# The last kv head's output-projection rows split into two 24-partition loads and one small load, in a one-core decode kernel

## The chip, the core and the metric

The kernel runs on one core of one Trainium2 chip. The metric is the device time of one execution in microseconds (us). The kernel before takes 124.86 us, the median of three runs (124.79 to 124.87).

## The reference

One decode step for a batch of 8, with one token each (D = 512). Cut to what matters:

```python
xn = layernorm(x)
q  = (xn @ wq)                        # 32 query heads of 128, 8 kv heads (4 query heads each)
k, v = last 1024 rows of each cache   # W = max(256, Sk // 4), Sk = 4096
s  = (softmax(q k^T / sqrt(128)) v) @ wo              # [8, 4096] @ [4096, 512]
g  = silu((gelu(xn @ w_gate) * (xn @ w_up)) @ w_down) # F = 1792
out = x + s * g
```

All inputs are bf16. The caches are read only in their last 1024 rows, 32 MB for K and V together; the weights are about 14 MB. The output is 8 x 512.

## The kernel before

Everything is written out in one order by hand, and every engine runs its own instructions in that order.

**Loads.** All large loads are issued on SyncE's queue (SP) into the slots of one ring of 19 tiles of 128 partitions x 8 KB (`slot`, L81). `load_rows` (L84 to 92) brings wq in four loads, w_gate and w_up in two each, w_down in two. `load_set` (L94 to 103) brings one set, that is four batches of one kv head, of K or of V, 1 MB. There are 16 sets. `load_wo` (L105 to 114) brings the 512 rows of wo that belong to one kv head: partition p gets rows 4p to 4p+3 of the head, so the four rows of a partition are one run of memory. Eight counters take turns for the landings, so a load is issued only when the load eight before it has landed.

**Order of the loads.** wq, w_gate, w_up, K of sets 0 to 2, w_down, then V and K in turns, and at the end wo: seven heads in one load of 512 KB each, the eighth in two halves of 256 KB (L473 and 474).

**Work.** The main loop (L434 on) is in quarters of a set. TensorE transposes K (L292), VectorE and ScalarE copy it out of PSUM by turns (L297, L299), TensorE forms the scores (L309), the maxima are taken out (L318 to L343), ScalarE takes the exponentials (L349), TensorE forms the sums and the product with V (L354, L371), and VectorE scales the result into `oT` (L377): partition = element d of a head, then kv head h, query head j, batch b.

**pick and put.** wo's rows for a head are in order 128j + d. With `load_wo`, partition p holds rows 4p + r, so `oT` has to be reordered to match. `pick` (L388 to 396) does it for one kv head with four matmuls by 0/1 matrices `picks[r]` into a PSUM tile `m_ps`; `put` (L398 to 404) copies the four blocks of 32 partitions into `oR`. Both run for each head one step after its last product with V, for the last head after everything else.

**Constants.** GpSimd builds the 0/1 matrices ahead of everything by `select` (L132, an affine select). Its last work is to clear `xq_sb` (L180); four small loads of x on ScalarE's queue (L183) wait for that.

**End.** After the loop VectorE clears `s_ps` (L472), and TensorE multiplies `oR` with wo (L479): for each of the four r of each head, four matmuls, one for each block of 128 output columns, each into its own block of 32 partitions of `s_ps`. 128 matmuls in all. Then two VectorE operations (L488, L489) and four small stores (L492).

Of the kernel before, what the change touches and what calls it, by code (L numbers as in the profile page):

```python
# [9 lines left out]
ALU = mybir.AluOpType  # L10
AX = mybir.AxisListType
BF16 = mybir.dt.bfloat16
FP32 = mybir.dt.float32
# [4 lines left out]
def kernel(  # L18
# [13 lines left out]
    nc = tc.nc  # L32

    B, Sq, D = A_x.shape
    Hkv, Sk, Dh = A_k_cache.shape[1], A_k_cache.shape[2], A_k_cache.shape[3]
    Hq = A_wq.shape[1] // Dh
    rep = Hq // Hkv
# [6 lines left out]
    P = nc.NUM_PARTITIONS  # L44
# [10 lines left out]
    QT = 4  # L55
    CQ = NCH // QT
    NQB = D // 128
    NEG = -1.0e30
    SHK = 64 + G

    consts = ctx.enter_context(tc.tile_pool(name="consts", bufs=1))
    ring = ctx.enter_context(tc.tile_pool(name="ring", bufs=19))
    kT_pool = ctx.enter_context(tc.tile_pool(name="kT_pool", bufs=8))
    pT_pool = ctx.enter_context(tc.tile_pool(name="pT_pool", bufs=6))
    small = ctx.enter_context(tc.tile_pool(name="small", bufs=3))
    rows = ctx.enter_context(tc.tile_pool(name="rows", bufs=1))
# [6 lines left out]
    ps_m = ctx.enter_context(tc.tile_pool(name="ps_m", bufs=1, space=PSUM))  # L73
# [7 lines left out]
    def slot():  # L81
        return ring.tile([P, SET], BF16, name="slot")

    def load_rows(w, r0, n, per, name):  # L84

        t = slot()
        cols = w.shape[1]
        nc.sync.dma_start(  # L88
            out=t[:, 0 : n * cols],
            in_=w.rearrange("(p k) n -> p k n", p=P)[:, r0 : r0 + n, :],  # L90
        )
        return t[:, 0 : n * cols].rearrange("p (k n) -> p k n", k=n)
# [12 lines left out]
    def load_wo(h, r0, n):  # L105

        t = slot()
        nc.sync.dma_start(
            out=t[:, 0 : n * D],
            in_=A_wo[h * rep * Dh : (h + 1) * rep * Dh, :].rearrange(  # L110
                "(p r) n -> p r n", r=rep
            )[:, r0 : r0 + n, :],
        )
        return t[:, 0 : n * D].rearrange("p (r n) -> p r n", r=n)

    wq_tiles = [load_rows(A_wq, k, 1, NDC, "wq") for k in range(NDC)]


    ident = consts.tile([P, P], BF16, name="ident")
    identf = consts.tile([P, P], FP32, name="identf")  # L120
    ones = consts.tile([P, P], BF16, name="ones")
    zsrc = consts.tile([P, P], FP32, name="zsrc")
# [9 lines left out]
    def select(out, in_, op, fill, base, pattern, cm):  # L132
        nc.gpsimd.affine_select(
            out=out, in_=in_, compare_op=op, fill=fill, base=base,
            pattern=pattern, channel_multiplier=cm,
        )
# [14 lines left out]
    for r in range(rep):  # L151
        t = consts.tile([P, P], BF16, name=f"pick{r}")
# [3 lines left out]
    for i in range(3):  # L156
        t = consts.tile([P, NC], BF16, name=f"shift{i}")
# [9 lines left out]
        shifts.append(t)  # L167


    stats = rows.tile([B, nc.vector.BN_STATS_DIM], FP32, name="stats")  # L170
    nc.vector.bn_stats(out=stats, in_=x_sb)
    mv = rows.tile([B, nc.vector.BN_AGGR_DIM], FP32, name="mv")
# [9 lines left out]
    for q in range(NQB):  # L182
        nc.scalar.dma_start(  # L183
            out=xq_sb[32 * q : 32 * q + B, :],
            in_=x_flat[:, q * 128 : (q + 1) * 128],
# [4 lines left out]
        out=xhat, in0=x_sb, scalar1=mv[:, 0:1], scalar2=rstd[:, 0:1],  # L190
# [10 lines left out]
    qT = rows.tile([P, Hkv, B, rep], BF16, name="qT")  # L201
    oT = rows.tile([P, Hkv, rep, B], BF16, name="oT")
    oR = rows.tile([P, Hkv, rep, B], BF16, name="oR")
    hT = rows.tile([P, NFC, B], BF16, name="hT")
    g_sb = rows.tile([P, 128], FP32, name="g_sb")

# [2 lines left out]
    for k in range(NDC):  # L209
        w = wq_tiles[k]  # L210
        for m in range(Hq):
            nc.tensor.matmul(  # L212
                q_ps[:, m, :], w[:, 0, m * Dh : (m + 1) * Dh], xnT[:, k, :],
                start=(k == 0 and m == 0), stop=(k == NDC - 1 and m == Hq - 1),
                skip_group_check=True,
            )
    nc.vector.tensor_copy(
        out=qT, in_=q_ps.rearrange("p (h j) b -> p h b j", j=rep)
# [5 lines left out]
    for w, src in enumerate((B_w_gate, B_w_up)):  # L224
        for k0 in range(0, NDC, KW):
            wt = load_rows(src, k0, KW, NDC, "gu")
            wv = wt.rearrange("p k (f j) -> p k j f", j=NFC)
            for j in range(NFC):
                for k in range(KW):
                    nc.tensor.matmul(  # L230
                        gu_ps[:, j, w, :], wv[:, k, j, :], xnT[:, k0 + k, :],
                        start=(w == 0 and k0 == 0 and j == 0 and k == 0),
                        stop=(w == 1 and k0 + k == NDC - 1 and j == NFC - 1),
                        skip_group_check=True,
# [54 lines left out]
    def transpose_quarter(s, i):  # L289
        ps = ps_kT.tile([P, CQ * P], BF16, name="kT_ps")  # L290
        for c in range(CQ):
            nc.tensor.transpose(  # L292
                ps[:, c * P : (c + 1) * P], K[s][:, i * CQ + c, :], ident
            )
        t = kT_pool.tile([P, CQ * P], BF16, name="kT")
        if i % 2 == 0:
            nc.vector.tensor_copy(out=t, in_=ps)  # L297
        else:
            nc.scalar.activation(out=t, in_=ps, func=ACT.Copy)  # L299
        kT[s, i] = t  # L300

    def score_quarter(s, i):
        h, b0 = s // NB, (s % NB) * G
        if i == 0:
            sc[s] = ps_sc.tile([P, NCH, NC], FP32, name="sc")
        t = kT.pop((s, i))
        q = qT[:, h, b0 : b0 + G, :].rearrange("p b j -> p (b j)")
        for c in range(CQ):
            nc.tensor.matmul(  # L309
                sc[s][:, i * CQ + c, :], t[:, c * P : (c + 1) * P], q,  # L310
                start=(i == 0 and c == 0), stop=False, skip_group_check=True,
            )
# [28 lines left out]
    def exponentials(s):  # L341
        r = shifts[s % 3]
        nc.tensor.matmul(  # L343
            sc[s].rearrange("p c n -> p (c n)"), spread[0:SHK, :],
            r[0:SHK, :].unsqueeze(1).to_broadcast([SHK, NCH, NC]),
            start=False, stop=True, skip_group_check=True,
# [38 lines left out]

    picked = {}

    def pick(h):  # L388
        ps = ps_m.tile([P, rep, rep, B], FP32, name="m_ps")
        for r in range(rep):  # L390
            nc.tensor.matmul(  # L391
                ps[:, r, :, :].rearrange("p j b -> p (j b)"), picks[r],
                oT[:, h, :, :].rearrange("p j b -> p (j b)"),
                start=(r == 0), stop=(r == rep - 1), skip_group_check=True,
            )
        picked[h] = ps

    def put(h):  # L398
        ps = picked.pop(h)
        for j in range(rep):  # L400
            nc.vector.tensor_copy(  # L401
                out=oR[32 * j : 32 * j + 32, h, :, :],
                in_=ps[32 * j : 32 * j + 32, :, j, :],
            )
# [15 lines left out]
    def fetch(kind, s):  # L420
        while True:
            k, i = pending.pop(0)
            if k == "K":
                K[i] = load_set(A_k_cache, i)
            elif k == "V":
                V[i] = load_set(A_v_cache, i)
            else:
                n = NFC // 2
                down_tiles.append(load_rows(B_w_down, i * n, n, NFC, "wd"))
            if (k, i) == (kind, s):  # L430
                return

    LV = 4 * (AHEAD - 1) + 2
    for t in range(QT * NS + LV + QT + 3):  # L434
        s, i = divmod(t, QT)
        if s < NS:
            if i == 0:
                fetch("K", s)
            transpose_quarter(s, i)
        s2, i2 = divmod(t - 2, QT)  # L440
        if 0 <= s2 < NS:
            score_quarter(s2, i2)
            if i2 == QT - 1:
                maxima(s2)
        u = t - 6
        if u >= 0 and u % QT == 0 and u // QT < NS:
            max_rows(u // QT)
        u = t - 8
        if u >= 0 and u % QT == 0 and u // QT < NS:
            exponentials(u // QT)  # L450
        u = t - 11
        if u >= 0 and u % QT == 0 and u // QT < NS:
            sums(u // QT)
        s3, i3 = divmod(t - LV, QT)
        if 0 <= s3 < NS:
            if i3 == 0:
                fetch("V", s3)
            value_quarter(s3, i3)
        u = t - LV - 2 * QT - 1
        if u >= 0 and u % (2 * QT) == 0:  # L460
            pick(u // (2 * QT))
        if u > 0 and u % (2 * QT) == 1:
            put(u // (2 * QT))
        if t == QT * AHEAD + 1:
            down(0)
        if t == QT * AHEAD + 3:
            down(1)
            gate()


    s_ps = ps_s.tile([P, 128], FP32, name="s")
    nc.vector.memset(s_ps, 0.0)  # L472
    parts = [(h, 0, rep) for h in range(Hkv - 1)]  # L473
    parts += [(Hkv - 1, 0, rep // 2), (Hkv - 1, rep // 2, rep // 2)]
    for h, r0, n in parts:
        w = load_wo(h, r0, n)
        for r in range(r0, r0 + n):
            for q in range(NQB):
                nc.tensor.matmul(  # L479
                    s_ps[32 * q : 32 * q + B, :], oR[:, h, r, :],  # L480
                    w[:, r - r0, q * 128 : (q + 1) * 128],
                    start=(h == 0 and r == 0), stop=(h == Hkv - 1 and r == rep - 1),
                    skip_group_check=True,
                )
    tmp = small.tile([P, 128], FP32, name="tmp", bufs=1)
    out_sb = small.tile([P, 128], BF16, name="out_sb", bufs=1)
    o_flat = out.flatten_outer_dims()
# [2 lines left out]
    for q in range(NQB):  # L490
        eng = nc.sync if q % 2 == 0 else nc.scalar
        eng.dma_start(  # L492
            out=o_flat[:, q * 128 : (q + 1) * 128], in_=out_sb[32 * q : 32 * q + B, :]
# [31 lines left out]
```

## Time and profile before

| What | Value |
|---|---|
| median of three runs | 124.86 us |
| the profiled execution | 124.77 us |
| its span in the profile | 123.0 us |
| DMA in the chain that ended last | 87% |
| read from HBM | 47.46 MB, 386 GB/s over the span |
| TensorE busy | 89.6 us (73%) |
| VectorE busy | 69.1 us (56%) |
| ScalarE busy | 45.9 us (37%) |
| GpSimd busy | 4.9 us (4%) |
| granted TensorE clock, mean | 0.936 |

Times inside the profile count from the span's start. The profiled execution's own time is 1.77 us longer than its span. The chain that ended last is followed back from the last instruction: a large share for DMA says that the end waits for loads. PE is TensorE's matmuls, PEld its weight loads, DVE VectorE, ACT ScalarE, POOL GpSimd, SP SyncE. A core has 16 DMA engines, and the DMA share is the mean over them.

### The profile page before, as it was taken

The numbers are of one execution on the slowest core, as the hardware profiler recorded it, in microseconds if no ns is written. First come the engines' busy times: TensorE is split into PE (matmuls) and PEld (weight loads), VectorE is DVE, ScalarE is ACT, GpSimd is POOL, SyncE is SP. The second block draws the span as 40 slices with busy tenths as digits, with TensorE's granted clock in tenths as the row PEclk, the third lists the DMA queues.
The fourth block names the chain that finished last, engine by engine and source line by source line (L and its number), as shares of the span: only waits on it lengthen the run. The fifth ranks groups of instructions, "written<-read, shape, count | busy, mean of one in ns | idle before, by whom it ended". The sixth has DMA issues, their size and how long they took to land.

```text
span 123.0 us, 4592 instructions
## 1 busy us (share of the span) xinstructions
PE 89.6 (73%) x2044; PEld 80.5 (65%) x2044; DVE 69.1 (56%) x218; ACT 45.9 (37%) x54; POOL 4.9 (4%) x21
## 2 busy tenths in 40 slices
PE   0243368868995799998979798767979779854840
PEld 0243358858984698988879697666968768643720
DVE  3400100043676547998787796669679689876010
ACT  4000000073583507567466355445536545510000
POOL 6800000000000000000000000000000000000000
PEclk9999999999999859999999999999999999995555
DMA  4999999999999999999999999999999999999720
GB/s 115 426 426 416 423 417 421 425 410 423 423 420 410 426 418 416 413 413 418 426 410 421 413 426 416 418 416 416 416 426 405 424 416 421 401 408 407 306 82 3
DMA packets 7508, 47.77 MB, mean 388 GB/s; under 512 B 952, under 2 KB 960, under 8 KB 2880
## 3 DMA queue, kind: packets, MB, share of 16 engines
q1 hardware_dynamic: 7376, 47.46, 93.7%
q8 instruction: 16, 0.26, 0.9%
q10 hardware_dynamic: 112, 0.02, 0.2%
q14 instruction: 4, 0.03, 0.1%
HBM read 47.46 MB, written 0.01 MB: 386 GB/s over the span
## 4 chain that ended last, share of the span: by engine, by line
DMA 87%; PE 8%; issue 1%; DVE 1%; SPq 1%; DVEq 0%
DMA slot<-in_A_k_cache_dram 49%; DMA slot<-in_A_wo_dram 23%; DMA slot<-in_B_w_up_dram 8%; DMA slot<-in_A_wq_dram 7%; PE kT_ps L292 3%; PE s L268 1%; PE sc L309 1%; PE o_ps L371 1%; SPq L88 1%; PE sc L343 0%; PE s L479 0%; DVE tmp L488 0%; DVE out_sb L489 0%; PE m_ps L325 0%; PE sum_ps L354 0%
## 5 line engine op out<-in xcount | busy, mean ns | idle before, releaser
L292 PE MATMUL kT_ps<-ident,slot 128*128 128x128 bf16 x512 | 41.9, 229 | 7.5 <-DMA slot<-in_A_k_cache_dram 6.0
L299 ACT ACTIVATE kT<-kT_ps 128x1024 bf16<-128x1024 bf16 x32 | 32.7, 1023 | 23.6 <-PE kT_ps L292 22.0
L292 PEld LDWEIGHTS <-slot 128*128 128x128 bf16 x512 | 31.8, 102 | 9.2 <-DMA slot<-in_A_k_cache_dram 7.5
L297 DVE COPY kT<-kT_ps 128x1024 bf16<-128x1024 bf16 x32 | 21.7, 679 | 9.7 <-PE kT_ps L292 9.7
L371 PEld LDWEIGHTS <-slot 128*128 128x128 bf16 x512 | 20.4, 96 | 7.9 <-issue 2.5
L371 PE MATMUL o_ps<-pT,slot 128*128 128x16 bf16 x512 | 22.0, 170 | 2.1 <-DVE oT L377 1.2
L309 PE MATMUL sc<-qT,kT 128*128 128x16 bf16 x512 | 22.5, 171 | 0.0
L309 PEld LDWEIGHTS <-kT 128*128 128x128 bf16 x512 | 19.9, 97 | 0.0
L349 ACT ACTIVATE pT<-sc 128x512 bf16<-128x512 f32 x16 | 9.6, 597 | 16.4 <-PE sc L343 16.3
L318 DVE TENSOR_REDUCE mx<-sc 128x16 f32<-128x512 f32 x16 | 11.1, 691 | 4.6 <-PE sc L309 4.3
L359 DVE TENSOR_REDUCE rec<-sum_ps 128x16 f32<-128x512 f32 x16 | 11.1, 691 | 3.9 <-PE sum_ps L354 3.5
L230 PE MATMUL sc<-xnT,slot 128*128 128x8 bf16 x112 | 7.4, 202 | 3.4 <-DMA slot<-in_B_w_gate_dram 2.7
L230 PEld LDWEIGHTS <-slot 128*128 128x128 bf16 x112 | 7.0, 159 | 3.7 <-DMA slot<-in_B_w_gate_dram 2.9
L241 ACT ACTIVATE z<-sc 128x112 f32<-128x112 f32 x1 | 0.3, 263 | 20.8 <-PE sc L230 20.8
L212 PE MATMUL sc<-xnT,slot 128*128 128x8 bf16 x128 | 4.1, 169 | 4.9 <-DMA slot<-in_A_wq_dram 4.9
L212 PEld LDWEIGHTS <-slot 128*128 128x128 bf16 x128 | 3.7, 104 | 5.3 <-DMA slot<-in_A_wq_dram 5.3
L354 PE MATMUL sum_ps<-pT,ones 128*128 128x512 bf16 x16 | 6.1, 379 | 0.5 <-issue 0.5
L401 DVE CAST oR<-m_ps 32x32 bf16<-32x32 f32 x32 | 5.8, 183 | 0.7 <-PE m_ps L391 0.4
L479 PE MATMUL s<-slot,oR 128*8 128x128 bf16 x128 | 4.3, 305 | 2.7 <-DMA slot<-in_A_wo_dram 1.5
L242 DVE TENSOR_SCALAR z<-z 128x112 f32<-128x112 f32 x1 | 0.2, 219 | 10.6 <-ACT z L241 10.6
L343 PE MATMUL sc<-shift,spread 68*128 68x512 bf16 x16 | 6.0, 376 | 0.2
L325 PE MATMUL m_ps<-identf,mx 128*16 128x128 f32 x16 | 4.5, 283 | 2.1 <-DVE mx L318 1.2
(58 smaller groups left out, 47.8 us busy)
## 6 DMA issues: line engine op xcount, KB each, us to landing
slot<-in_A_k_cache_dram SPq DMA_DIRECT2D x16, 1024.0 KB, 14.9
slot<-in_A_v_cache_dram SPq DMA_DIRECT2D x16, 1024.0 KB, 20.1
slot<-in_A_wq_dram SPq DMA_DIRECT2D x4, 1024.0 KB, 10.4
slot<-in_A_wo_dram SPq DMA_DIRECT2D x7, 512.0 KB
slot<-in_B_w_gate_dram SPq DMA_DIRECT2D x2, 896.0 KB
slot<-in_B_w_up_dram SPq DMA_DIRECT2D x2, 896.0 KB
slot<-in_B_w_down_dram SPq DMA_DIRECT2D x2, 896.0 KB
slot<-in_A_wo_dram SPq DMA_DIRECT2D x2, 256.0 KB, 9.4
```

The lines of the kernel that those rows point to most:

```text
L212: nc.tensor.matmul(q_ps[:, m, :], w[:, 0, m * Dh : (m + 1) * Dh], xnT[:, k, :], start=(k == 0 and m == 0), stop=(k == NDC - 1 and m == Hq ...
L230: nc.tensor.matmul(gu_ps[:, j, w, :], wv[:, k, j, :], xnT[:, k0 + k, :], start=(w == 0 and k0 == 0 and j == 0 and k == 0), stop=(w == 1 an ...
L292: nc.tensor.transpose(ps[:, c * P : (c + 1) * P], K[s][:, i * CQ + c, :], ident)
L297: nc.vector.tensor_copy(out=t, in_=ps)
L299: nc.scalar.activation(out=t, in_=ps, func=ACT.Copy)
L309: nc.tensor.matmul(sc[s][:, i * CQ + c, :], t[:, c * P : (c + 1) * P], q, start=(i == 0 and c == 0), stop=False, skip_group_check=True,)
L318: nc.vector.tensor_reduce(out=m, in_=sc[s].rearrange("p c n -> p n c"), axis=AX.X, op=ALU.max)
L343: nc.tensor.matmul(sc[s].rearrange("p c n -> p (c n)"), spread[0:SHK, :], r[0:SHK, :].unsqueeze(1).to_broadcast([SHK, NCH, NC]), start=Fal ...
L349: nc.scalar.activation(out=t, in_=sc.pop(s), func=ACT.Exp, scale=scale)
L354: nc.tensor.matmul(ps.rearrange("p c n -> p (c n)"), ones, pT[s].rearrange("p c n -> p (c n)"), start=True, stop=True,)
L359: nc.vector.tensor_reduce(out=t, in_=ps.rearrange("p c n -> p n c"), axis=AX.X, op=ALU.add)
L371: nc.tensor.matmul(o_ps[s].rearrange("p g j -> p (g j)"), V[s][:, c, :], pT[s][:, c, :], start=(c == 0), stop=(c == NCH - 1),)
```

## The change

The ring has 18 slots in place of 19, and a tile `wlow` of 64 partitions x 8 KB is added.

For the last head (`LAST`), the 128 rows of each query head j are divided: rows d = 0 to 31 and rows d = 32 to 127.

- `load_wo_low` loads rows 32 to 127 of all four j, three quarters of the head, in two loads of 24 partitions each: partitions 0 to 23 and 32 to 55 of `wlow`. Partition 32g + 4e + j holds the eight rows 32 + 48g + 8e to 39 + 48g + 8e of query head j, 8 KB in one run. The outer dimension of the source is e, six long.
- `load_wo_few` loads rows 0 to 31 of all four j, 128 rows of 1 KB, one on each partition of a ring slot.
- The order at the end is: heads 0 to 5 in one load each, the two low loads of the last head, head 6 in two halves, and the few rows of the last head.
- `pick_last` brings `oT` of the last head into the matching order with 36 matmuls in place of four: for the few rows and for each of the eight rows of a partition one matmul for each j, by a slice of `few` (132 columns) or of `spots[r]` (60 columns), 128 or 56 columns wide, that starts at column 3 - j. `put` then makes two copies in place of four: into the new tile `oL` (56 partitions x 64) and into `oR`.
- The product with wo has 148 matmuls in place of 128.
- GpSimd builds `few` and eight `spots`, and clears `wlow`, ahead of clearing `xq_sb`.

```diff
+    DF = 32
+    NE = 6
+    RL = (Dh - DF) // (2 * NE)
+    PL = 32 + rep * NE
+    LAST = Hkv - 1
-    ring = ctx.enter_context(tc.tile_pool(name="ring", bufs=19))
+    ring = ctx.enter_context(tc.tile_pool(name="ring", bufs=18))
...
+    def load_wo_few(h):
+        t = slot()
+        nc.sync.dma_start(
+            out=t[:, 0:D],
+            in_=A_wo[h * rep * Dh : (h + 1) * rep * Dh, :].rearrange(
+                "(j d) n -> d j n", j=rep
+            )[0:DF],
+        )
+        return t[:, 0:D].rearrange("p (r n) -> p r n", r=1)
+    wlow = rows.tile([P // 2, RL * D], BF16, name="wlow")
+    def load_wo_low(h):
+        t = wlow
+        rows_h = A_wo[h * rep * Dh : (h + 1) * rep * Dh, :].rearrange(
+            "(j d) n -> j d n", j=rep
+        )[:, DF:Dh, :]
+        for g in range(2):
+            nc.sync.dma_start(
+                out=t[32 * g : 32 * g + rep * NE, 0 : RL * D],
+                in_=rows_h[:, g * NE * RL : (g + 1) * NE * RL, :].rearrange(
+                    "j (e r) n -> e j (r n)", e=NE
+                ),
+            )
+        return t[0 : 32 + rep * NE, 0 : RL * D].rearrange("p (r n) -> p r n", r=RL)
...
+    few = consts.tile([P, P + rep], BF16, name="few")
+    nc.gpsimd.memset(few, 0.0)
+    select(
+        few[:, rep - 1 : P + rep - 1 : rep], zsrc[:, 0:DF], ALU.not_equal, 1.0, 0,
+        [[-1, DF]], 1,
+    )
+    spots = []
+    for r in range(RL):
+        t = consts.tile([P, PL + rep], BF16, name=f"spot{r}")
+        nc.gpsimd.memset(t, 0.0)
+        for g in range(2):
+            c0 = 32 * g + rep - 1
+            select(
+                t[:, c0 : c0 + rep * NE : rep], zsrc[:, 0:NE], ALU.not_equal, 1.0,
+                -(DF + NE * g * RL + r), [[-RL, NE]], 1,
+            )
+        spots.append(t)
+    nc.gpsimd.memset(wlow, 0.0)
...
+    oL = rows.tile([PL, RL, B], BF16, name="oL")
...
+    def pick_last(h):
+        ps = ps_m.tile([P, RL + 1, B], FP32, name="m_ps")
+        for r in [RL, *range(RL)]:
+            lo, n = (few, P) if r == RL else (spots[r], PL)
+            for j in range(rep):
+                nc.tensor.matmul(
+                    ps[0:n, r, :], lo[:, rep - 1 - j : n + rep - 1 - j], oT[:, h, j, :],
+                    start=(r == RL and j == 0), stop=(r == RL - 1 and j == rep - 1),
+                    skip_group_check=True,
+                )
+        picked[h] = ps
...
     def put(h):
         ps = picked.pop(h)
+        if h == LAST:
+            nc.vector.tensor_copy(out=oL[:, :, :], in_=ps[0:PL, 0:RL, :])
+            nc.vector.tensor_copy(out=oR[:, h, 0, :], in_=ps[:, RL, :])
+            return
...
-            pick(u // (2 * QT))
+            h = u // (2 * QT)
+            (pick_last if h == LAST else pick)(h)
...
-    parts = [(h, 0, rep) for h in range(Hkv - 1)]
-    parts += [(Hkv - 1, 0, rep // 2), (Hkv - 1, rep // 2, rep // 2)]
+    half = rep // 2
+    parts = [(h, 0, rep) for h in range(Hkv - 2)]
+    parts += [(LAST, 1, RL), (Hkv - 2, 0, half), (Hkv - 2, half, half), (LAST, 0, 1)]
+    done, total = 0, (Hkv - 1) * rep + RL + 1
     for h, r0, n in parts:
-        w = load_wo(h, r0, n)
-        for r in range(r0, r0 + n):
+        if h < LAST:
+            w, o = load_wo(h, r0, n), oR[:, h, r0 : r0 + n]
+        elif n == 1:
+            w, o = load_wo_few(h), oR[:, h, 0:1]
+        else:
+            w, o = load_wo_low(h), oL
+        for r in range(n):
             for q in range(NQB):
                 nc.tensor.matmul(
-                    s_ps[32 * q : 32 * q + B, :], oR[:, h, r, :],
-                    w[:, r - r0, q * 128 : (q + 1) * 128],
-                    start=(h == 0 and r == 0), stop=(h == Hkv - 1 and r == rep - 1),
-                    skip_group_check=True,
+                    s_ps[32 * q : 32 * q + B, :], o[:, r, :],
+                    w[:, r, q * 128 : (q + 1) * 128],
+                    start=(done == 0), stop=(done == total - 1), skip_group_check=True,
                 )
+            done += 1
```

## The prediction

> **What bounds the kernel now.** The chain that ended last comes first: DMA holds 87% of it, and it ends so (start us, us, what):
>
> ```profile
> 110.02 8.88 DMA slot<-in_A_wo_dram
> 118.89 0.04 issue
> 118.94 0.41 PE s L479 x8
> 119.35 0.02 issue
> 119.37 0.30 DVE tmp L488
> ```
>
> The last quarter-megabyte load of wo lands at 118.89, eight matmuls of 0.41 us follow, then the epilogue to 123.0. So the end moves only with the last landing, or when TensorE becomes later than it. The next view is the busy time by stretch near the end (us, PE, PEld, DVE, ACT, POOL busy with counts, clock, DMA share, GB/s):
>
> ```profile
> 114.00:115.00 1.00, 1.00 (x48) 1.00 (x40) 0.00 (x0) 0.00 (x0) 0.00 (x0) 0.50 1.01 391
> 115.50:116.00 0.50, 0.27 (x12) 0.08 (x1) 0.00 (x0) 0.00 (x0) 0.00 (x0) 0.50 0.66 262
> 116.00:117.00 1.00, 0.60 (x16) 0.40 (x16) 0.00 (x0) 0.00 (x0) 0.00 (x0) 0.50 0.54 213
> 117.00:118.00 1.00, 0.36 (x16) 0.36 (x16) 0.00 (x0) 0.00 (x0) 0.00 (x0) 0.50 0.54 191
> 118.00:118.50 0.50, 0.45 (x20) 0.23 (x9) 0.00 (x0) 0.00 (x0) 0.00 (x0) 0.50 0.17 61
> ```
>
> All 16 DMA engines work until 115, about half of them (0.54) until 118. Each has the same bytes of every load, so some lag by 3 us. The page's queues name a cause:
>
> ```profile
> q8 instruction: 16, 0.26, 0.9%
> q14 instruction: 4, 0.03, 0.1%
> ```
>
> The trace keeps every packet with start, length and size. On the data queue a packet starts 3 to 6 ns before the one ahead ends, so the records can be strung into 16 chains, one per engine (close chains can be swapped; no engine number is kept). Each 16 KB packet of q8 holds its chain for about 1.05 us, and the packet behind it takes 0.77 to 0.86 instead of 0.31: 1.5 us lost. They go round eight chains, and seven of these have two by the end. The four 8 KB packets of q14 cost 0.7 to 0.97 each: two hit one chain, the others one each. The last packets of the chains end at: 115.05 to 115.30 (five, untouched), 115.8 to 115.9 (two with one q14 packet), 116.59 (one q8), 117.10 (two q14), 118.08 to 118.48 (seven with two q8). 118.48 plus 0.46 to the waiting matmul is the 118.94 of the chain.
>
> **The change, part by part.**
>
> *Bytes per engine.* Packets of 8, 4 and 2 KB take 312, 159 and 84 ns. Before, after the sixth head (h5) each engine has 8 packets of 4 KB and 16 of 2 KB, 2.59 us with their completion writes. Now all have 16 of 2 KB (head 6 in halves) and 8 of 1 KB; six engines have besides 8 of 8 KB (two loads of 24 rows in six shares of four). The differences 153 and 75 ns halve with the size, so I put a 1 KB packet at 47 ns, 8 at 0.36 us; the ends are the 256-byte packets of x (18 ns, 0.14 us) and the 2 KB ones (0.67). Ten engines: 0.36 for 1.28, so 0.92 less. The six: 2.46 - 0.92 = 1.54 more.
>
> *Which six?* The 8-row load of x ran as eight packets of 1 KB on eight chains, and its followers' phases lie on the eight chains without q8 packets. A load in six shares should fall among those eight. Then: late chains 118.48 - 0.92 = 117.56; untouched 115.30 + 1.54 = 116.84; one q14 packet 115.86 + 1.54 = 117.40. The chain with two is the doubt: 116.18 if not among the six, 118.64 if it is. The Trainium skill ("DMA: Bandwidth & Descriptors", section on why a DMA increments its semaphore by 16) says that a copy runs on the largest k up to 16 that divides both slowest dimensions, on the lowest-numbered engines: six here, and the trace's eight x packets agree.
>
> *TensorE at the end.* Start us, us, engine, line, operands, count:
>
> ```profile
> 110.57 0.83 PE L371 MATMUL o_ps<-pT,slot 128*128 128x16 bf16 x24
> 112.12 0.27 PE L391 MATMUL m_ps<-oT,pick 128*128 128x32 bf16 x4 [0.72 <-DVE oT L377]
> 112.43 0.79 DVE L401 CAST oR<-m_ps 32x32 bf16<-32x32 f32 x4 [0.36 <-PE m_ps L391]
> 113.25 0.17 DVE L472 MEMSET s<- 128x128 f32 x1
> 16.36 1.84 PE L230 MATMUL sc<-xnT,slot 128*128 128x8 bf16 x28 [2.34 <-DMA slot<-in_B_w_gate_dram]
> ```
>
> The last head's pick grows from 4 pairs of weight load and matmul to 36. At 112.12 the four start 27 ns apart. Strided weights (L230) go at 60 ns apiece at full clock, and 120 if half clock doubles that. So a pair costs p = 27 to 120 ns; unit-stride weights are nearest to the first row, and I take 27, with the other end kept. The copies behind: one of 64 columns and one of 8 against four of 32 (186 ns each; 16 columns of oT take 170, so 0.21 + 0.17, 0.40 with the gap) in place of 0.79. Product matmuls then start at 112.12 + 35p + 0.86 (0.23 matmul to copy, 0.40, memset 0.17, 0.06 gaps): 113.93 at p = 27, against 113.47. They run in groups of four, 0.107 us a group; 148 in place of 128 are 37 groups. The last group could start 36 groups (3.84) later, 117.77. The data come at 117.56 + 0.46 = 118.02. So the load still decides, up to p = 35 ns. The Trainium skill ("TensorE: Matmul & The Clock Gate", LDWEIGHTS) prices a weight load at columns/1.2 ns, and gives fast loading to 128 weights only; 56 columns would be an estimate of 47 ns, which lets TensorE decide; no row here has that width.
>
> *Its clock* can soften that. Stretches between possible switches:
>
> ```profile
> 38.87:42.29 3.42, 2.07 (x49) 1.94 (x50) 1.88 (x4) 1.64 (x3) 0.00 (x0) 1.00 1.01 422
> 42.29:45.70 3.41, 2.99 (x60) 2.71 (x60) 1.38 (x7) 0.30 (x1) 0.00 (x0) 0.50 1.02 416
> 45.70:49.11 3.41, 3.41 (x102) 3.03 (x101) 2.56 (x8) 2.23 (x4) 0.00 (x0) 1.00 1.01 423
> 113.97:117.38 3.41, 2.40 (x84) 2.01 (x77) 0.00 (x0) 0.00 (x0) 0.00 (x0) 0.50 0.72 278
> ```
>
> The granted clock switches at 42.29, 45.70 and 110.55, twenty such stretches later. 2.07 us busy was followed by half clock, 2.99 by full, 2.40 by half again. With more matmuls 113.97 to 117.38 holds 2.7 to 3.3 us, so full clock from 117.38 is likely but not sure; then 0.054 a group, and the load decides up to about p = 50.
>
> *The last group.* One in place of two behind the last landing: 0.11 less.
>
> *At nothing.* Ring of 18: a slot's earlier reader ends at least 12 us before it would be issued, as the issues go eight loads ahead of the landings. Two more issues on SP (0.33 us each): SP only waits there, on the landing eight loads earlier; the last load is issued at about 112.5, and the late chains reach it at 117.2. GpSimd's new constants: selects of 0.2 to 0.5 us and memsets of 0.2, and one of 4096 columns (128 columns 204 ns, one column 98: 0.83 ns a column, 3.5 us), together some 9 us. Behind them the xq memset and, on ACT, four xq loads move from 6.3 to about 16; ACT's next work is at 24.80, so 8 us of cover. GpSimd's longer program may bring one more q14 packet (up to 0.97 on a chain): 116.84 + 0.97 = 117.81, at most 0.25 past the late chains. The 104 extra TensorE instructions move the last two q8 packets earlier; the second (117.38 before) may reach the chain that had one: 116.59 - 0.92 + 1.5 = 117.17, under 117.56.
>
> **The sum.** The last group starts at 118.02 in place of 118.94, and is 0.11 shorter: -1.03 us. The profiled execution took 124.77 (span 123.0, 1.77 around it): 123.74; the median of the runs is 124.86, 0.09 above it: **123.85**. From the 1 KB packet's ends and full clock behind the last landing (0.1) its own range is 123.5 to 124.15.
>
> **Rivals.**
> 1. *TensorE takes the end*, at half clock with p between 35 and 60. At p = 50 the last group starts at 112.12 + 1.75 + 0.86 + 3.84 = 118.57, ends 0.32 later, 118.89 against 119.37: -0.48, **124.4**. For it: 56-wide weights at odd offsets are unlike any row. Against: L391's 27 ns, the clock.
> 2. *The chain with two q14 packets is among the six.* 118.64 + 0.46 = 119.10, last group to 119.42 against 119.37: +0.05, **124.9**. For it: six of eight places; against: nothing in the trace numbers the engines.
> 3. *Slower: the odd-offset weights load slowly.* From p = 64 TensorE ends later than before (112.12 + 35p + 0.86 + 3.84 + 0.32 = 119.37). At 120 ns: 121.34, +1.97, **126.8**. For it: L230's 60 ns; against: those weights are strided, these not.
> 4. *The shares don't stay on six engines.* Then every engine has the old bytes, and only the shorter last group gains: **124.75**. The Trainium skill (the DMA page's rules for kernel authors) says that transfers to disjoint partition halves spray over all 16 engines, which would make it so; the eight chains of x speak against it.
>
> **How the numbers follow.** Forecast 0.42, rival 1 0.18, rival 2 0.25, rival 3 0.11, rival 4 0.04. Faster by over 0.2% (0.25 us, about what a measurement of this kernel can tell): forecast and rival 1, 0.60. Within it: rivals 2 and 4, 0.29. Slower: 0.11. The range leaves out rival 3 and the tails: 123.5 to 125.0.
>
> **What would show it.** After: DMA share falls from 115 on as before, but ends near 117.6; the last landing near 118.0 and a wait for it ahead of the last four matmuls. Rival 1: no such wait, matmuls in one run until the end. Rival 2: a share near 0.06 (one engine) for the last microsecond. Rival 3: the 36 pairs take over 2.2 us. Rival 4: share 0.54 until about 118. The prediction is wrong if the q8 packets move to other engines, or if 8 KB packets on few engines take other than 312 ns.

## The result, and the profile after

The changed kernel is slower: 125.81 us (125.78 to 126.04, four runs) against 124.87 us (124.79 to 124.87, four runs) for the kernel before on the same chip. The ratio is 1.0078, with a 95% interval of 1.0064 to 1.0093. The profiled execution took 125.80 us (span 124.0), 1.03 us more than before's 124.77.

The end of the chain of waits of the changed kernel (start us, us, what):

```profile
108.56 9.95 DMA wlow<-in_A_wo_dram
118.51 0.14 issue
118.64 1.85 PE s L560 x41
120.52 0.30 DVE tmp L569
```

The chain still comes from a load. The profile follows it back to the low rows (`wlow`), which land at 118.51 with 52 matmuls behind them (the chain counts 41); the starts of these matmuls, below, show later landings in between. The epilogue starts at 120.52 in place of 119.37.

The busy time by stretch (us, PE, PEld, DVE, ACT, POOL busy with counts, clock, DMA share, GB/s):

```profile
116.00:117.00 1.00, 1.00 (x45) 0.89 (x37) 0.00 (x0) 0.00 (x0) 0.00 (x0) 0.50 0.74 279
117.00:118.00 1.00, 0.86 (x32) 0.57 (x23) 0.00 (x0) 0.00 (x0) 0.00 (x0) 0.50 0.26 98
118.00:119.00 1.00, 0.36 (x16) 0.39 (x20) 0.00 (x0) 0.00 (x0) 0.00 (x0) 0.50 0.10 39
119.00:120.00 1.00, 1.00 (x44) 0.70 (x33) 0.00 (x0) 0.00 (x0) 0.00 (x0) 0.50 0.13 31
```

Before, the DMA share was 0.54 until 118 and 0.17 in the half microsecond behind it. Now it falls to 0.26 in the stretch from 117, and to 0.10 and 0.13 behind 118: one or two engines of 16 work alone for the last 2 us. The packets say which. Strung into 16 chains, the ten without shares end at 117.6 or sooner, and the prediction had 117.56 for the latest of them. The six with shares are these (packets of 8 KB take 309 to 328 ns):

| Chain among the six | sixth head's last packet | low rows' last 8 KB packet | last small packet |
|---|---|---|---|
| no instruction packet | 112.47 | 114.98 | 116.6 |
| one q14 packet (three chains) | 113.13 to 113.42 | 115.63 to 115.92 | 117.2 to 117.6 |
| two q14 packets | 114.38 | 116.88 | 118.52 |
| **two q8 packets** | **115.52** | **118.01** | **119.65** |

So one of the six is a chain that carries two 16 KB instruction packets of q8. What TensorE does meanwhile (start us, us, engine, line, operands, count, idle time before it and what ended it):

```profile
112.81 1.57 PEld L449 LDWEIGHTS <-spot 128*56 128x56 bf16 x32
115.04 2.82 PE L560 MATMUL s<-slot,oR 128*8 128x128 bf16 x96 [0.57 <-DVE s L545]
118.64 1.02 PE L560 MATMUL s<-wlow,oL 56*8 56x128 bf16 x32 [0.78 <-DMA wlow<-in_A_wo_dram]
119.59 0.88 PE L560 MATMUL s<-slot,oR 128*8 128x128 bf16 x20
```

The 32 pairs of the 56-wide pick took 1.57 us, 49 ns a pair; the products started at 115.04. But TensorE then waits 0.78 us for the low rows, so it has time to spare. It also waits for the last landing: the last small packet ends at 119.65, the load's semaphore is full at 120.15, and the last four matmuls start at 120.19, 0.04 behind it. Before, the last eight started at 118.94, 0.05 behind the landing at 118.89. The profile prints no idle time there, because the matmuls ahead are still in flight (0.31 us each). At its pace of 0.107 us a group TensorE would have started the last four at about 120.03. So the late chain sets the end, and TensorE has 0.16 us to spare there.

### The profile page after: what moved, and what is told of

Read it like the earlier page. It is cut to its first block, busy times and chain, and to the rows that moved or that the text cites. A ratio compares the mean times of both kernels' runs of the same rounds, so it can differ in the third digit from the quotient of the medians.

```text
span 124.0 us, 4743 instructions
## 1 busy us (share of the span) xinstructions
PE 90.4 (73%) x2096; PEld 81.5 (66%) x2096; DVE 68.5 (55%) x216; ACT 45.9 (37%) x54; POOL 12.1 (10%) x48
## 4 chain that ended last, share of the span: by engine, by line
DMA 77%; POOL 8%; PE 7%; SPq 2%; issue 2%; DVE 1%; POOLq 0%; DVEq 0%
DMA slot<-in_A_k_cache_dram 47%; DMA slot<-in_A_v_cache_dram 16%; DMA wlow<-in_A_wo_dram 8%; DMA xq_sb<-in_A_x_dram 4%; PE kT_ps L348 3%; POOL wlow L222 3%; POOL spot L166 2%; DMA x_sb<-in_A_x_dram 2%; PE s L560 1%; SPq L102 1%; POOL pick L166 1%; POOL shift L166 1%; SPq L93 1%; PE sc L365 1%; PE o_ps L427 1%
## 5 line engine op out<-in xcount | busy, mean ns | idle before, releaser
L348 PE MATMUL kT_ps<-ident,slot 128*128 128x128 bf16 x512 | 40.8, 226 | 5.8 <-DMA slot<-in_A_k_cache_dram 4.0
L473 DVE CAST oR<-m_ps 32x32 bf16<-32x32 f32 x28 | 5.1, 182 | 0.3
```

What stands on the lines that cost most here:

```text
L348: nc.tensor.transpose(ps[:, c * P : (c + 1) * P], K[s][:, i * CQ + c, :], ident)
```

## The experiments

**Theory 1**: DMA engines that carry instruction packets are late, and the six shares fall on engines 0 to 5, among which is a late one. **Theory 2** in the expectations is that the loss lies in the order and the work of the end (when the low rows come, the longer pick, the constants) and not in the engines. Each set of runs is compared with runs of the kernel before on the same chip: 124.79 us in sections 1, 2, 3 and 5, 124.76 in sections 4, 6 and 7, 124.62 (another chip) in section 8 and for the first run of section 9, 124.69 (a third chip) for the other three of section 9.

### 1. Numbering the engines

Before's kernel with 15 tiny loads of k rows, k = 1 to 15, one behind each set of V; the lengths of their packets tell them apart:

```diff
+    def mark(k):
+        n = 67 + 16 * k
+        nc.sync.dma_start(out=mk[0:k, 320 * k : 320 * k + n], in_=A_wo[0:k, 0:n])
```

> The kernel before, with 15 tiny loads added on the same queue, one behind each V set from 1 to 15: the k-th has k rows (of 166, 198, 230, ... bytes), so its packets should fall on k engines, and the engine that the k-th has and the one before has not is engine k-1. Theory 1 (two of the six engines that the low loads ran on are engines that instruction packets hold up): among the engines 0 to 5 one is about 3.0 us behind the untouched ones by the 15th V load (two packets of 16 KB) and one about 1 to 2 us behind (packets of 8 KB). Theory 2 (TensorE's longer pick and the 53 products behind the low loads set the end, and which engines carry them matters little): the engines 0 to 5 are all within 1 us of each other. Time 124.9 by both.

125.05 us, one run. Start of each packet, us from the span's start; one column is one engine, since consecutive marks are 4.98 to 5.00 us apart on each:

| k | | | | | | |
|---|---|---|---|---|---|---|
| 3 | 50.529 | 50.086 | 50.230 | | | |
| 4 | 55.514 | 55.073 | 55.214 | 56.194 | | |
| 5 | 60.504 | 60.066 | 60.204 | 61.187 | 59.897 | |
| 6 | 65.494 | 65.056 | 65.198 | 66.181 | 64.900 | 66.784 |

Each k adds one engine and keeps the others; the trace has no engine numbers, so engine k - 1 is here the one that the k-th mark adds. That a load of k shares runs on the k lowest-numbered engines is the rule of the Trainium skill that the prediction cited ("DMA: Bandwidth & Descriptors"), and the trace agrees up to k = 15 in that there are k packets on nested sets of engines. The sixth engine, engine 5, comes 1.9 us behind engine 4 at 66.8 and 3.2 us behind the untouched ones at 108.4: it carries q8 packets. So do 6 and 9 to 14; engine 3 carries two of q14; 0, 1, 2, 4, 7, 8 and 15 carry no 16 KB packets (15 by elimination, since no mark reaches it). The prediction had put all eight late chains outside the first eight. Theory 1 holds so far.

### 2. The low rows first

The changed kernel with the two low loads issued ahead of all other wo loads, the products in the same order:

```diff
+    low = load_wo_low(LAST)
     for h, r0, n in parts:
...
-            w, o = load_wo_low(h), oL
+            w, o = low, oL
```

> The changed kernel with the two low loads issued ahead of the eight-head wo loads instead of behind the sixth; the order of the products is unchanged. Theory 1: each engine still has the same bytes, so the late engine among the six ends its last packet of the small load at the same 119.65 and the time stays at 125.8 (125.6 to 125.9). Theory 2: the low rows are there long before they are needed, nothing waits behind them, and the end falls to that of the ten other engines, last landing about 118.0: 124.1.

126.17 us, ratio 1.0111 (1.0096 to 1.0126). Theory 2's 124.1 falls: the time is not in when the low rows come. The late engine's last packet ends at 119.75, where it did (119.65), since its bytes are the same. Theory 1 expected 125.8; the 0.36 on top is the order: the heads behind the low rows all come 2.5 us later on engine 5. Now the sixth head is what TensorE waits for:

```profile
118.65 0.60 PE L561 MATMUL s<-slot,oR 128*8 128x128 bf16 x16 [0.66 <-DMA slot<-in_A_wo_dram]
119.18 1.02 PE L561 MATMUL s<-wlow,oL 56*8 56x128 bf16 x32
```

Behind that wait stand 68 matmuls in place of 52, 16 x 27 = 0.43 us more. In this run TensorE ends last: the last load has landed at 120.25, and the last matmul starts at 120.53 without a wait between the last 20.

### 3. Sixteen shares

The low rows in one load on partitions 0 to 63, sixteen shares of four packets of 6 KB, `NE = 16` and one group; the few rows stay as they were, 1 KB on each partition:

```diff
-    NE = 6
-    RL = (Dh - DF) // (2 * NE)
+    NE = 16
+    NG = 1
+    RL = (Dh - DF) // (NG * NE)
```

> The changed kernel with the low rows in one load of sixteen shares on partitions 0 to 63 (six rows of 1 KB to a partition) in place of two loads of six shares: every engine has the bytes of before again, and the pick has 28 pairs. Theory 1: the late engines end as in the kernel before, only the last group of products is shorter: 124.75 (124.6 to 124.9). Theory 2: the pick is still seven times as long and 44 products stand behind the low load: 125.4.

126.91 us, ratio 1.0164 (1.0148 to 1.0179). Both miss. The stretch in which these rows come:

```profile
114.00:115.00 1.00, 0.69 (x13) 0.68 (x13) 0.27 (x2) 0.00 (x0) 0.00 (x0) 0.50 0.96 209
```

The engines are busy (0.96) but move 209 GB/s, not the 391 that the kernel before moved in this stretch. A 6 KB packet that ran by itself took 234 ns; the median was 332, the longest 502. The shares of engines e and e + 8 lie on partitions 32 apart here. The Trainium skill ("SBUF — State Buffer", Door 1) says that partitions 32 apart share a port, which fits; no run here took that alone away. As a control this run is spoiled, so the next takes 128 partitions.

### 4. The same on all 128 partitions

One load of 3 KB a partition, `NE = 32`, three rows of matmuls in place of eight (`RL = 3`), the order as in the changed kernel.

> The low rows of the last head go into all 128 partitions, 3 KB each, in one load over sixteen engines (the few rows and the order of loads stay as in the changed kernel; three rows of matmuls instead of eight, 112 + 16 products). Every engine then has the bytes of the kernel before, and no two shares meet on a port. Theory 1 (the six shares fall on engines that are already late from instruction packets): the two-packet engines end at about 118.5 again as in the kernel before, the end comes one group of products sooner (-0.11 us): 124.7 us, within 0.2% of before. Theory 2 (the order at the end, the longer pick with wide weights, or the constants cost the time, whatever the shares): about 125.4 or more.

124.98 us, ratio 1.0018 (1.0009 to 1.0027). The load of sixteen shares leaves 0.22 of the 0.94 us that the change lost; 3 KB packets had a median of 125 ns. In its trace the last landing is at 118.86, where before's was (118.89), and the epilogue at 119.18, 0.19 sooner than before, as theory 1 has it. The run is yet 0.28 us longer than expected, and that lies outside the span: its profiled execution took 2.11 us more than its span, before's 1.78. Its trace has a q14 instruction packet at 124.32, 1.57 us behind the span's end. Only two other runs have such a packet, both with three shares on 96 partitions (section 9), and they too take 1.91 and 2.04 us more than their spans; no run isolates it.

### 5. More instruction packets

The kernel before with 64 idle pairs of weight load and matmul behind each of the four wq loads, 512 instructions in all, whose output nobody reads:

```diff
+        idle = ps_m.tile([P, B], FP32, name="m_ps")
+        for m in range(64):
+            nc.tensor.matmul(idle, ident, xnT[:, 0, :], start=True, stop=True)
```

> The kernel before with 256 more pairs of weight load and matmul on TensorE behind the four wq loads, where it waits for DMA; their results are used nowhere. 512 more instructions should bring two more 16 KB instruction packets. Theory 1: two engines get a third such packet (1.5 us each), their chains end 1.5 us later, and the time is 126.3 (126.0 to 126.5). The rival for the cause of the lag (some engines are slower by themselves, the instruction packets are incidental): no change, 124.9.

126.27 us, ratio 1.0113 (1.0096 to 1.0130). The page's queue line has two more 16 KB packets, with no byte of data more:

```profile
q8 instruction: 18, 0.29, 1.0%
```

One chain now ends at 119.997, the others at 118.55 or sooner: a third packet costs its chain about the same 1.5 us as each of the first two. The expectation had two such chains; the last q8 packet starts at 119.08, too late for a second. The idle matmuls lie beside the wq loads, far ahead of the end, so it is the packets that cost.

### 6. Four and eight shares

Half of the head in two loads of four shares (`NE = 4`, 8 KB packets, engines 0 to 3), and three quarters in two loads of eight (`NE = 8`, 6 KB packets, engines 0 to 7); the rest in the small load.

> Half of the last head in two loads of four shares of 8 KB packets (engines 0 to 3), the other half as a small load of 2 KB per partition. Of these four engines only engine 3 is late, by its two VectorE instruction packets; no engine with 16 KB packets has a share. Theory 1: the engines with 16 KB packets have 0.61 us less after head 5 than in the kernel before (16 of 2 KB and 8 of 2 KB in place of 8 of 4 KB and 16 of 2 KB) and end at about 117.8; engine 3 ends at about 118.8 and alone sets the end: tmp at about 119.75, 125.1 us (124.9 to 125.3). If eight-KB shares as such cost the time, and not the engine that they fall on, it stays at 125.8.

124.97 us, ratio 1.0018 (1.0009 to 1.0028). Right: engine 3 alone is late, and its last packet ends at 118.78 (the prediction's rival 2 put a chain of its kind at 118.64 and the time at 124.9). The epilogue is 0.24 us later than before, as the median is 0.21; shares of 8 KB as such cost nothing beyond what engine 3's lag accounts for.

> Three quarters of the last head as in the changed kernel, but in two loads of eight shares, 6 KB packets, on engines 0 to 7, 48 KB of them each in place of 64 KB. Theory 1: engines 5 and 6, with two 16 KB packets each, set the end; each has 8 x 78 ns = 0.62 us less than engine 5 in the changed kernel: last packets at about 119.0, tmp at about 119.9, 125.2 us (125.0 to 125.4), with a DMA share near 0.13 (two engines) in the last microsecond. A rival without engine numbers (any engine with a share is late by its bytes alone) would put the end before 118.4, and the time at 124.3.

125.92 us, ratio 1.0092 (1.0077 to 1.0106). Two chains, and only two, are late: their last packets end at 119.61 and 119.62, the third latest at 118.38. These are engines 5 and 6. The stretches show the two as shares of 0.16:

```profile
117.00:118.00 1.00, 0.78 (x32) 0.49 (x20) 0.00 (x0) 0.00 (x0) 0.00 (x0) 0.50 0.46 171
118.00:119.00 1.00, 0.41 (x20) 0.44 (x24) 0.00 (x0) 0.00 (x0) 0.00 (x0) 0.50 0.16 58
119.00:120.00 1.00, 0.86 (x32) 0.45 (x24) 0.00 (x0) 0.00 (x0) 0.00 (x0) 0.50 0.16 45
```

Which engines was right, the time 0.7 us too low: the two ended the sixth head at 116.08, where engine 5 had been at 115.52. Most of that half microsecond is not engine 5's: the whole stream is later in this run, its first wo packet starting at 105.21 for 104.73 and the earliest chain with shares ending the sixth head at 112.86 for 112.47. The lag against that chain is 3.23 us for 3.05.

### 7. Three shares, on engines without 16 KB packets

Three eighths of the head in two loads of three shares; 64 rows of each j as a load of 2 KB a partition, the last 16 as a small one. The products of heads 0 to 3 go ahead of the last pick and put:

```diff
+            if h == LAST:
+                product(0)
+                product(1)
+                pick_last(h)
+                product(2)
+                product(3)
```

> Three eighths of the last head in two loads of three shares of 8 KB packets, so on engines 0, 1 and 2 alone, which have no 16 KB packets and one 8 KB instruction packet each at most; 64 rows of each query head as a load of 2 KB per partition, and 16 rows as a last load on 64 partitions. TensorE's products of heads 0 to 3 move ahead of the last pick. Theory 1: the engines with two 16 KB packets have 0.46 to 0.9 us less behind head 5 and end at about 117.7 to 118.0; the three with shares at about 117 to 117.7; the end about 0.6 us sooner than in the kernel before: 124.2 us (123.9 to 124.5). If shares on few engines cost time of themselves: 125 or more. Rival of TensorE: if the wide pick still ends last, no wait for a load stands ahead of the last products, and the time is 124.5 to 125.

125.11 us, ratio 1.0025 (1.0013 to 1.0038). The data came as expected: the last packet ends at 117.85, 0.61 sooner than before. The gain was taken by TensorE, the rival's way, and 0.1 us beyond even that rival's 124.5 to 125. The chain:

```profile
113.44 1.80 PE m_ps L455 x44
115.24 0.84 PE s L533 x25
116.07 0.62 issue
116.69 3.16 PE s L533 x93
119.85 0.02 issue
```

No load stands in it behind 113: 44 pairs of pick and 156 products at half clock are too many. In the middle of one head's products it stops for 0.62 us. In this run's trace such pauses stand at TensorE's instructions 1729, 1985, 2241, 2497, 2753, 3009 and 4033, all multiples of 256 apart, and each ends 1.36 to 1.47 us behind the end of a q8 packet: so it looks as if TensorE waits here for its own program. That is argued from place and time; no run isolates it.

### 8. Two controls for the work on TensorE

The same move of the products in the changed kernel, and in the kernel before:

> The changed kernel with the products of heads 0 to 3 moved ahead of the last pick and put, so that TensorE has about 1.7 us less to do behind the wide pick; loads, shares and their order unchanged. Theory 1 (the end is the landing of engine 5's packets, 118.0 for the low rows and 119.65 for the last small ones): TensorE waits longer for the low rows, and the time stays at 125.8 (125.6 to 125.9). If the 36 pairs of the pick cost the time: about 125.0.

125.92 us, ratio 1.0100 (1.0082 to 1.0118). The wide pick costs nothing: with less work behind it TensorE only waits longer, 0.99 in place of 0.78 us, for the same rows.

```profile
118.93 1.02 PE L526 MATMUL s<-wlow,oL 56*8 56x128 bf16 x32 [0.99 <-DMA wlow<-in_A_wo_dram]
```

> The kernel before with the products of heads 0 to 3 moved ahead of the last pick, no other change: the control for the moved products in the runs with three shares. Theory 1 (the last landing decides before): 124.8, no change. If moved products themselves gain: 124.4 or less; if they lose by the half clock: 125.1 or more.

124.67 us, ratio 1.0005 (0.9995 to 1.0014): no change, since the last landing decides there too.

### 9. Three shares with little work, and where the ring lies

The three shares as rows 64 to 127 of j = 1 to 3, 2 KB on each of 96 partitions, so that the pick has 15 pairs and the product 132 matmuls:

```diff
+            out=t[:, :],
+            in_=A_wo[h * rep * Dh : (h + 1) * rep * Dh, :].rearrange(
+                "(j d) n -> j d n", j=rep
+            )[1:rep, DF:Dh, :].rearrange("j (d r) n -> j d (r n)", r=RL),
```

> As the run with three shares (its last packet ended at 117.85, but TensorE ended at 119.85, at half clock, with a pause of 0.62 us behind an instruction packet), with less work for TensorE at the end: the 192 rows of the three shares are rows 64 to 127 of query heads 1 to 3, 2 KB on each of 96 partitions in one load, so the last pick has 15 pairs in place of 44 and the product 132 matmuls in place of 156. The data should end at 117.85 again (0.2 later if 2 KB packets of two engines meet), 118.3 at the waiting matmul, four matmuls behind it: tmp at about 118.65 against 119.37 before. Theory 1 (engines 0 to 2 have the time to spare, and TensorE alone took it back): 124.1 us (123.9 to 124.4). If shares on few engines cost time in some other way: 124.9 or more.

123.77 us, ratio 0.9929 (0.9913 to 0.9945). That looks like theory 1's gain, but the trace says otherwise: the first wo packet starts at 103.45, and in all runs so far at 104.5 to 105.3. The whole stream is faster from the start: 99% of the 8 KB packets took 309 ns to within one (mean 312.2), where before most spread from 309 to 319 (median 312, mean 315.9). This kernel has other constants ahead of the ring in memory, and so its 18 slots begin at byte 20736 of a partition, a multiple of 256 (worked out from the tiles' sizes; the trace has no addresses). In the kernel before they begin at 20032, 64 past one, in the changed kernel at 21344, 96 past; none of the other runs has a multiple. Three runs separate the two causes, each with one unused tile, which moves every buffer behind it; the first of them:

```diff
+    pad = consts.tile([P, 96], BF16, name="pad")
     ident = consts.tile([P, P], BF16, name="ident")
```

> The kernel before with an unused tile of 192 bytes ahead of the constants, so that the ring begins at byte 20224 of the partition, a multiple of 256, in place of 20032; no instruction is changed. Theory A (the place of the ring sets the duration of its packets): all 8 KB packets 309 ns, the wo packets start 1.2 to 1.35 us sooner, 123.4 us (123.2 to 123.7), as fast as or faster than three shares on 96 partitions (123.77), which then gained nothing by the shares. Theory B (three shares gained): 124.6, no change.

**123.03 us**, ratio 0.9868 (0.9855 to 0.9881). With not one instruction changed the kernel before is 1.66 us faster: 8 KB packets 309 ns again, the first wo packet at 103.59. The two-packet chains gain besides, since a 16 KB packet now takes 0.88 to 0.97 us for 1.02 to 1.10 (the last one, 1.15 for 1.23, left out); theory A's 123.2 to 123.7 had counted the 8 KB packets alone. This is the fastest version of all. The Trainium skill ("DMA: Bandwidth & Descriptors", section on how a descriptor splits into AXI transactions) says that a transaction has to start at a multiple of 256 bytes, and that a descriptor which starts elsewhere begins at the boundary below and fetches unused bytes that still cost time. It gives no price, and it speaks of reading, where here the written side moved; the packets fit it, with 309 ns against a median of 312.

> The changed kernel with an unused tile of 160 bytes ahead of the constants, so that the ring begins at 21504, a multiple of 256, in place of 21344. Theory A: the whole stream is 1.2 us sooner, engine 5 is as late against the others as before: 124.6 us (124.4 to 124.8), still about 1 us slower than the kernel before with the same ring. Theory B: 125.8, no change. If the lag of engine 5 came from the place of the ring: 123.5.

124.14 us, ratio 0.9960 (0.9947 to 0.9972). The changed kernel gains as much by the place of its ring (125.81 to 124.14), more than the 1.2 us that theory A took, and is then 124.14 - 123.03 = 1.11 us slower than before with the same ring. The loss is not in the place. In its last two stretches two engines and then one work alone, as in the first run (share 0.06 is one of 16):

```profile
116.00:117.00 1.00, 0.19 (x10) 0.04 (x2) 0.00 (x0) 0.00 (x0) 0.00 (x0) 0.50 0.12 47
117.00:118.00 1.00, 1.00 (x36) 0.78 (x40) 0.00 (x0) 0.00 (x0) 0.00 (x0) 0.50 0.06 24
```

> Three shares on 96 partitions with an unused tile of 64 bytes ahead of the constants: the ring begins at 20800, 64 past a multiple of 256, as in the kernel before. Theory A: 124.9 us (124.6 to 125.1), no faster than before. Theory B (the shares gained, not the ring): 123.8.

125.71 us, ratio 1.0081 (1.0068 to 1.0095): off the multiple, three shares on 96 partitions lose 1.0 us. So the three shares on 96 partitions gained nothing; against the kernel before with its ring at a multiple they lost 0.74 (123.77 - 123.03, on two chips whose times before were 124.62 and 124.69). In the stretch of these rows the rate falls as in the third experiment:

```profile
114.00:115.00 1.00, 0.72 (x28) 0.54 (x20) 0.16 (x2) 0.00 (x0) 0.00 (x0) 0.50 1.08 289
```

205 of its 480 packets of 2 KB took over 100 ns, where they take 84 alone. The shares of engines 0 and 1 lie on partitions 32 apart here. That this is the cause is argued from the third experiment, not shown; theory A's 124.9 was 0.8 too low for it.

## Why the prediction was wrong

The sign was wrong and the time was out of the range.

- **"Which six?" failed.** The prediction placed the six shares "among those eight" chains that carry no q8 packets, from the phases of the followers of x's 8-row load. The marks show that the lowest six engines are 0 to 5, and that engine 5 carries two q8 packets. By the prediction's own terms that chain would end at 118.48 + 1.54 = 120.02; it ended at 119.65, so the last group started at 120.19 and not at 118.02. It had told the chains apart by the phases of the packets behind x's load; what misled it there stays open. Rival 2 saw the same danger but for the lesser chain: engine 3 with its two q14 packets is among the six as well and ended at 118.52, against 118.64 forecast.
- **The last group** was right. One group of four stands behind the last landing: from its start to the epilogue it is 0.33 us, before 0.43 for two, so 0.10 less (0.11 taken). With the start 1.25 later (120.19 for 118.94) the epilogue is 1.15 later; the rest of the execution is 0.12 shorter, which makes the 1.03 us of the profiled run.
- **Bytes per engine** was right: the chains without shares end by 117.6, as worked out; 8 packets of 1 KB took 0.343 us (0.36 taken).
- **The pick**: p was 49 ns, not 27. The figure of 47 that the prediction worked out from the Trainium skill was the better one. Products began at 115.04, not 113.93, but the price was hidden: section 8 took work from behind the pick and gained nothing. Rival 1's mechanism was present, and not on the path.
- **The clock** didn't switch to full at 117.38; it was 0.50 to the end.
- **At nothing** held: GpSimd was busy 12.1 us in place of 4.9, and a fifth q14 packet came, at 12.18, far from the end. The chain of waits does run back through GpSimd's constants (8% of the span) and the small loads of x, but the stream of loads was not later for it: the first wo packet started at 104.73, before at 104.83.

What the bytes freed on ten engines could have given was worth little in any case: three shares on engines without 16 KB packets ended the data 0.61 us sooner (section 7), and TensorE, at half clock, took that back.

## What to carry to other kernels

A load in few shares went to the same few engines every time here, so number the late engines by tiny marks before giving bytes to some: two of the first eight carried two 16 KB packets each. Where a kernel is bound by its loads, look at the distribution of its packets' durations first, and at where the buffers begin: 192 unused bytes gave 1.3%, more than any edit of the order. And a variant that changes the size of constants moves every buffer behind them, so a gain seen with it needs a control with the buffers in the old place.

## What the runs showed of the hardware that was not expected

- The place of the ring: 8 KB packets of 309 ns in the median at a multiple of 256 bytes, in three runs, against 311 to 313 at 32, 64, 96, 128, 160 or 192 past it: 1.66 us over the kernel, packets of other sizes included (section 9).
- TensorE paused at seven instructions that lie multiples of 256 apart, each time behind a q8 packet: 0.58 to 0.86 us a time in section 7's run, one of them in the last 8 us.
- Partitions 0 to 63 written by 16 engines: packets of 6 KB 332 ns in the median (section 3), against 235 where eight engines wrote them (section 6).
